# Later stores, other scratch rows and moved normalisations in a fused linear-attention and SwiGLU gradient kernel

## The chip, the cores and the metric

The kernel runs on one core of one Trainium2 chip, as one program with one launch. The metric is the device time of that program in microseconds, as the median of several runs. One further execution was taken by the hardware profiler; all views of the profile come from it.

## What is computed

The reference is one transformer block with all of its gradients. With S = 2048 tokens of width D = 640, 32 heads of 20, and a feed-forward width F = 1728, in bf16:

```python
phi = lambda t: where(t > 0, t + 1, exp(t)) + 1e-6
q, k, v = split_heads(LN(x) @ wqkv)            # LN has no weights
kv, z   = sum_s phi(k)[s] v[s]^T, sum_s phi(k)[s]
h       = x + ((phi(q) @ kv) / (phi(q) . z + 1e-6)) @ wo
y       = LN(h)
h2      = h + ((silu(y @ w_gate) * (y @ w_up)) @ w_down)
```

out_0 is h2. For a given grad_out, the outputs out_1 to out_6 are the gradients of x, wqkv (640x1920), wo, w_gate, w_up (640x1728 each) and w_down (1728x640). In what follows a name that begins with d is the gradient of the thing behind the d.

## The kernel before

**Tiles and stages.** Tokens are cut into 16 tiles of 128 rows; "tile t" means one of these, and a pair is two of them. The program has these stages, at about these times of the profiled execution:

- 0 to 141 us: the first layer norm, q and k with phi, the products that stand for kv and wo (Yt, KVT, W2), then h and the second layer norm. phi(q) is kept in DRAM as scr_pq, and the reciprocal of the denominator per token and head stays in SBUF as rall.
- 141 to 440 us: four feed-forward groups g of 448, 448, 448 and 384 columns, at 141, 214, 288 and 377 us. A group first makes gate and up (pg L792, pu L797) and their gradients pair by pair. Its gradients go transposed to scr_dT through the three "stg" buffers of the pool `small`. Then `dw_group` (L668) makes the weight gradients of those columns. The one of w_down is made transposed and stored to scr_dwdT.
- 440 to 558 us: the pair loop (L1032 to L1109), eight pairs from the last of the tokens' gradients to the attention's input, some 15.6 us each.
- 558 to 600 us: the tail behind that loop (L1110 to L1163), with the first products of G (`gt_part`).
- 600 to 627 us: the last products of G, the q part of the gradient of wqkv, and wk2 (L1227). 627 to 735 us: dk and dxn (L1280 to L1327), which end in out_1.
- 735 to 815 us: the output stage (L1453 to L1543), h2 by pairs of tiles, with the small gradients of wo and of the v part of wqkv (`dwo`, `dwv`, queue `small_q`) put between.

**Who sets the order.** Inside a `tc.manual_schedule(...)` block, the engines that it names run in the order in which the code is written; elsewhere a tile scheduler picks the order by priority and by which buffers are free. Each engine works off its own list in order, and a DMA is issued from the list of the engine that starts it, so an engine that waits for one DMA's input holds all its later DMAs. `tc.issue_after(x)` holds an instruction back in its list until behind x. Buffers come from pools: the four large strips (tag "S"), five of tag "B", three small "stg" ones, `work` (6) and `workC` (7) of one row of 640, and four PSUM tiles.

**phi(q)/den.** For G the kernel needs phi(q) times rall for all 16 tiles, as scr_pqs. `pq_load` (L635) loads tiles of scr_pq, `pq_norm` (L640) multiplies and stores. The table PQ (L646) says in which group's dw_group this is done (L729 to L750): from group g, n tiles from t0. The first five go through buffers of the feed-forward pool, further ones through stg. Before, groups 0, 1 and 2 do five, five and six tiles.

**The pair loop.** Pair p works on tiles 2p and 2p+1. The products p1, p3, p5, p6 and their relatives give the gradient of the layer norm's output (seven products where eight would do the plain way, with sums of blocks made by DVE). `ln_sum`, `ln_dot`, `ln_b` and `ln_c` (L941 to L960) do the layer norm's gradient one pair later, on tiles q2 = 2p-2 and q1 = 2p-1. `ln_c` ends with a POOL DMA that adds its result into dh1 (L957) and an SP DMA that reads that tile back transposed (dh1T, L960). `dp_mm` (L967) multiplies dh1T by W2T; `dp_a` (L975) and `dp_b` (L987) turn the result dp into dq, on tiles h-2 and f, three pairs behind. They need phi(q) again, which `load_q` (L962) loads into a stg buffer from POOL. Two tiles of scr_dwdT per pair are read back transposed on SP (dwd, L1080, buffers of workC) and stored to out_6 from POOL at the end of the same pair (L1105). Spare rows of the two tiles of transposed w_gate and w_up (`wgT`) serve as scratch: dy1 and rows pr, rx and junk.

**The tail.** Five tiles of dp work are left. They use two sets of scratch rows (L1129), so that one tile's first half runs beside the other's second half:

```python
prs, rxs = [dy1[0], pr], [junk, rx]     # dy1 and pr, rx are rows of wgT
```

`gt_part` (L907) gives the first column tiles of G = (dh1)^T pqs, over tiles t0 to t1, for one half of the columns and then for the other. `xn_act` (L999) scales rows of x, reloaded into hn (L1109, L1128), to the normalised x, on ACT, 12 tiles all told, all of them in the tail. Behind the tail wqkvT, which takes the place of one of the two wgT tiles (xnT_r takes the other), is loaded by 16 SP transposes (L1182 to L1188), held behind the last dh1T, and xnT_r by four POOL loads (L1189).

**The output stage.** Pass p of its loop (L1475) does the products of pair p and finishes pair p-1, and ends with one item of small_q except in pass 2; the rest of small_q is done behind the loop (L1522). The first item is a dwo, the other five are dwv, which need the transposes of scr_Yt into Y (L1483).

## Time and profile before

| | |
|---|---|
| time, median of 3 runs | 810.02 us (806.59 to 817.07) |
| the profiled execution: time, span | 816.33 us, 814.6 us |
| TensorE matmuls (PE) busy | 783.7 us, 96% |
| TensorE weight loads (PEld) busy | 498.8 us, 61% |
| VectorE (DVE) busy | 576.5 us, 71% |
| ScalarE (ACT) busy | 331.9 us, 41% |
| GpSimd (POOL) busy | 212.2 us, 26% |
| DMA, mean over the span | 209 GB/s |
| TensorE clock granted, mean | 0.987 |

The span is what the profiler saw of the core, from the first to the last instruction; the time has a little more around it. Weight loads run beside the matmuls. SyncE (SP) only issues DMAs here and is not counted as busy. In a timeline a row has its start in us, the busy time, the engine, the line and operation with output and input, how many instructions were merged, and in square brackets the idle time before it and what ended that. In the list of waits the numbers are the total in us, how often, and the longest one; "SPq" and "POOLq" are the DMA issues of those engines.

### The profile page before, as it was taken

To read this page: it belongs to the slowest core of one execution; us is meant where nothing else is said; L and a number is where in the kernel's file an instruction comes from. 1 tells how busy PE (TensorE), PEld (TensorE's weight loads), DVE (VectorE), ACT (ScalarE), POOL (GpSimd) and SP (SyncE) were. 2 spreads that over 40 slices of the span, in tenths; PEclk is the share of its full clock that TensorE was granted. 3 is DMA by queue.
4 is the path that set the end of the run, shared out by engine and by line. 5 is a ranking of instruction groups with operands and counts; after the bars stand their busy time and mean duration, and the time that the engine had idled before them with its cause. 6 is when DMAs were issued, how large, how long until landed. Compare 5 with 4: busy or idle time off the path is not lost.

```text
span 814.6 us, 13702 instructions
## 1 busy us (share of the span) xinstructions
PE 783.7 (96%) x5243; PEld 498.8 (61%) x5243; DVE 576.5 (71%) x1005; ACT 331.9 (41%) x490; POOL 212.2 (26%) x362
## 2 busy tenths in 40 slices
PE   9999999999999989999999999995895999999888
PEld 7776566555555545555666777773674777776555
DVE  7989988985696758757977679987561366626663
ACT  7962532840481145305701446645542133333010
POOL 4600057312311410123142133224521111123220
PEclk9999999999999999999999999998998999999989
DMA  9899999999799988995998799988669989999992
GB/s 256 173 231 317 181 260 245 262 260 229 180 225 225 182 239 215 255 184 137 215 235 240 218 204 199 249 188 232 138 115 240 164 170 170 171 248 221 203 219 82
DMA packets 291123, 170.62 MB, mean 209 GB/s; under 512 B 242396, under 2 KB 278365, under 8 KB 291056
## 3 DMA queue, kind: packets, MB, share of 16 engines
q1 hardware_dynamic: 268912, 99.56, 61.9%
q0 software_dynamic: 19248, 64.85, 28.1%
q10 hardware_dynamic: 2896, 5.33, 1.9%
q8 instruction: 41, 0.67, 0.4%
q14 instruction: 26, 0.21, 0.1%
HBM read 52.92 MB, written 56.28 MB: 134 GB/s over the span
## 4 chain that ended last, share of the span: by engine, by line
PE 84%; DMA 8%; SPq 3%; DVE 2%; ACT 2%; issue 1%; POOL 0%; POOLq 0%; ACTq 0%; DVEq 0%
PE ps_dw L871 10%; PE ps_dxn L1319 8%; PE pu L797 7%; PE ps_wa L687 7%; PE pg L792 7%; PE ps_dhn L935 6%; PE ps_dm L420 5%; PE ps_dwqk L1238 4%; PE ps_dhc L935 4%; PE ps_kq L308 4%; PE ps_oa L1389 3%; PE ps_dk L110 3%; PE ps_y L511 3%; PE ps_a L574 3%; PE ps_wc L687 2%; DMA dwd<-scr_dwdT 2%
## 5 line engine op out<-in xcount | busy, mean ns | idle before, releaser
L935 PEld LDWEIGHTS <-cols 128*128 128x128 bf16 x624 | 61.0, 98 | 24.2 <-issue 0.5
L792 PE MATMUL pg<-wgu,hnT 128*128 128x448 bf16 (+1 forms) x320 | 63.6, 346 | 1.2 <-DMA wgu<-in_B_w_gate_dram 1.2
L797 PE MATMUL pu<-wgu,hnT 128*128 128x448 bf16 (+1 forms) x320 | 63.6, 346 | 1.2 <-DMA wgu<-in_B_w_up_dram 1.2
L871 PE MATMUL ps_dw<-m_s,dh 128*128 128x448 bf16 (+1 forms) x320 | 60.4, 346 | 0.0
L1319 PEld LDWEIGHTS <-ring 128*128 128x128 bf16 x480 | 47.0, 98 | 18.2
L1319 PE MATMUL ps_dxn<-wqkvT,ring 128*128 128x320 bf16 x320 | 51.3, 299 | 0.0
L792 PEld LDWEIGHTS <-hnT 128*128 128x128 bf16 x320 | 31.2, 98 | 28.5 <-DMA wgu<-in_B_w_gate_dram 1.7
L797 PEld LDWEIGHTS <-hnT 128*128 128x128 bf16 x320 | 31.2, 98 | 28.5 <-DMA wgu<-in_B_w_up_dram 1.6
L871 PEld LDWEIGHTS <-dh 128*128 128x128 bf16 x320 | 31.3, 98 | 27.1
L420 PE MATMUL ps_dm<-wdT,dh2T 128*128 128x448 bf16 (+1 forms) x240 | 46.5, 344 | 0.0
L420 PEld LDWEIGHTS <-dh2T 128*128 128x128 bf16 x320 | 31.0, 98 | 25.1
L813 ACT ACTIVATE dd<-pg 128x896 bf16<-128x896 f32 (+1 forms) x32 | 28.5, 891 | 42.4 <-PE pg L792 42.4
L308 PE MATMUL ps_kq<-wqk,xnT 128*128 128x320 bf16 x320 | 44.8, 299 | 0.4 <-DMA xnT<-xn 0.3
L833 POOL DMA_DIRECT2D scr_m<-m_s x16 | 12.1, 756 | 125.4 <-DVE m_s L825 125.4
L1238 PEld LDWEIGHTS <-hn 128*128 128x128 bf16 x320 | 31.4, 99 | 12.8 <-issue 0.3
L308 PEld LDWEIGHTS <-xnT 128*128 128x128 bf16 x320 | 31.0, 98 | 12.8 <-DMA xnT<-xn 0.6
L687 PEld LDWEIGHTS <-S 128*128 128x128 bf16 x256 | 25.0, 98 | 21.7
L683 DVE TENSOR_TENSOR dd<-dd 128x3584 bf16<-128x3584 bf16 (+1 forms) x12 | 23.1, 1954 | 18.9 <-PE ps_wa L687 18.9
L110 PE MATMUL ps_dp<-mats,dh1T 128*128 128x320 bf16 x160 | 25.7, 310 | 10.0 <-DMA dh1T<-dh 8.0
L140 POOL TENSOR_SCALAR lnv<-mv 128x1 f32<-128x1 f32 x32 | 11.9, 373 | 89.4 <-DVE mv L136 73.5
L148 DVE CUSTOM_DVE_ANT_0 lb_a<-lb_dy,hn 128x640 bf16<-128x640 bf16 x16 | 13.2, 825 | 30.4 <-ACT lb_dy L146 30.4
L825 DVE TENSOR_TENSOR m_s<-m_s,dd 128x896 bf16<-128x896 bf16 (+1 forms) x32 | 19.4, 605 | 17.0 <-ACT m_s L818 17.0
(245 smaller groups left out, 1768.7 us busy)
## 6 DMA issues: line engine op xcount, KB each, us to landing
scr_dT<-stg SPq DMA_DIRECT2D x48, 224.0 KB, 2.9
cols<-scr_dT POOLq DMA_DIRECT2D x6, 1728.0 KB, 10.5
scr_m<-m_s POOLq DMA_DIRECT2D x12, 448.0 KB, 4.5
pq<-scr_pq POOLq DMA_DIRECT2D x32, 160.0 KB, 5.5
cols<-scr_dT ACTq DMA_DIRECT2D x2, 1728.0 KB, 10.9
scr_dT<-stg SPq DMA_DIRECT2D x16, 192.0 KB, 2.4
scr_pq<-pqa SPq DMA_DIRECT2D x4, 640.0 KB, 4.4
scr_xnT<-xnT SPq DMA_DIRECT2D x4, 640.0 KB, 5.1
```

Source lines behind the costliest of these rows:

```text
L110: nc.tensor.matmul(ps[:, ci, :320], lhsT=lhs(k), rhs=rhs(k, *NCH[ci]), start=(start and k == 0), stop=(stop and k == n - 1))
L308: nc.tensor.matmul(ps[:, ci, :320], lhsT=xnT[:, t, k, :], rhs=wqk[:, k, w0 + n0:w0 + n1], start=(k == 0), stop=(k == DT - 1))
L420: nc.tensor.matmul(ps[:, c, :w], lhsT=dh2T[:, kt, (t + c) * P:(t + c + 1) * P], rhs=wdT[:, kt, o:o + w], start=(kt == 0), stop=(kt == DT - 1))
L511: nc.tensor.matmul(ps[:, ci, :320], lhsT=xn[:, t, i * P:(i + 1) * P], rhs=pk[:, t, n0:n1], start=(t == 0), stop=(t == ST - 1))
L687: nc.tensor.matmul(out, lhsT=lhs[:, t, :], rhs=rhs[:, t, :], start=(first and t == 0), stop=(t == 7), skip_group_check=not first)
L792: nc.tensor.matmul(pg[:, c, :w], lhsT=hnT[:, kt, (t + c) * P:(t + c + 1) * P], rhs=wg[:, kt, 0:w], start=(kt == 0), stop=(kt == DT - 1))
L797: nc.tensor.matmul(pu[:, c, :w], lhsT=hnT[:, kt, (t + c) * P:(t + c + 1) * P], rhs=wg[:, kt, w:2 * w], start=(kt == 0), stop=(kt == DT - 1))
L813: sig = nc.scalar.activation(out=dg, in_=pg[:, :, :w], func=ACT.Sigmoid)
L871: nc.tensor.matmul(ps[:, c, :w], lhsT=lhs(t), rhs=rhs(t), start=(t == 0), stop=(t == ST - 1))
L935: nc.tensor.matmul(out, lhsT=lhs[:, k, :], rhs=rhs[:, k, :], start=(first and k == 0), stop=(k == HKG - 1), skip_group_check=not first)
L1238: nc.tensor.matmul(ps[:, ci, :320], lhsT=xn_r[:, t, i * P:(i + 1) * P], rhs=dq[t // 8][:, t % 8, n0:n1] if which == 0 else dk[:, t, n0:n1] ...
L1319: nc.tensor.matmul(ps[:, ci, :320], lhsT=lhs[:, i, :], rhs=rhs[:, i, n0:n1], start=(k == 0 and i == 0), stop=(k == 2 and i == DT - 1))
```

## The change

Five edits, in the order of the program:

1. phi(q)/den: group 1 does no tiles any more, group 2 does eight (5 to 12). Tiles 13 to 15 are loaded in pair 0 of the pair loop and multiplied and stored in pair 1, through stg buffers and with plain POOL DMAs.
2. The two dW_down stores of a pair move into the next pair, behind the first `ln_c` there (`store_dwd`); the last pair's go behind the first `ln_c` of the tail.
3. `xn_act` for tiles 0 to 5 moves into the last three pairs, two tiles each; 6 to 11 stay in the tail.
4. The tail's scratch rows prs and rxs are now three rows of the strip that dq's first half lies in (where the pair loop keeps s1, u2 and u3) and junk. For the first column tile of G, `gt_part` goes four token tiles at a time, alternating between the two halves of the columns.
5. In the output stage pass 3 does no item of small_q either, so that each dwv from there comes one pass later, and one more is left for behind the loop.

```diff
--- before.py
+++ after.py
@@ -632,18 +632,18 @@
 
         pq_in = {}
 
-        def pq_load(ts, own=True):
+        def pq_load(ts, own=True, dma=pool_store):
             for t in ts:
                 pq_in[t] = flat("pq") if own else small.tile([P, D], BF16, name="pq", tag="stg", bufs=3, padded_shape=[P, 7 * P])[:]
-                pool_store(pq_in[t], scr_pq_v[:, t, :])
-
-        def pq_norm(ts):
+                dma(pq_in[t], scr_pq_v[:, t, :])
+
+        def pq_norm(ts, dma=pool_store):
             for t in ts:
                 pq = pq_in.pop(t)
                 nc.vector.tensor_tensor(out=hb(pq), in0=hb(pq), in1=bc(rall[:, t, :]), op=ALU.mult)
-                pool_store(scr_pqs_v[:, t, :], pq)
-
-        PQ = {0: (0, 5), 1: (5, 5), 2: (10, 6)}
+                dma(scr_pqs_v[:, t, :], pq)
+
+        PQ = {0: (0, 5), 2: (5, 8)}
 
         wg_t = {}
 
@@ -904,9 +904,9 @@
     dh1 = dh2
     gts = {}
 
-    def gt_part(ps, i, t0, t1):
-        for ci, (n0, n1) in enumerate(NCH):
-            for t in range(t0, t1):
+    def gt_part(ps, i, t0, t1, by=ST):
+        for ci, (n0, n1), t in [(ci, n, t) for a in range(t0, t1, by) for ci, n in enumerate(NCH)
+                                for t in range(a, min(a + by, t1))]:
                 nc.tensor.matmul(ps[:, ci, :320], lhsT=dh1[:, t, i * P:(i + 1) * P], rhs=pqs_tm[:, t, n0:n1],
                                  start=(t == 0), stop=(t == ST - 1))
 
@@ -1001,6 +1001,12 @@
                 nc.scalar.activation(out=hn[:, t, :], in_=hn[:, t, :], func=ACT.Identity, scale=rstd1[:, t:t + 1],
                                      bias=nmr1[:, t:t + 1])
 
+        def store_dwd(p):
+            for i in (2 * p - 2, 2 * p - 1):
+                if i >= 0:
+                    r0 = i * P
+                    nc.gpsimd.dma_start(out=out_6[r0:min(r0 + P, F), :], in_=dwds.pop(i)[:min(P, F - r0), :])
+
         def rs(p, r):
             t = 2 * p + 1 - r
             return rstd2[:, t:t + 1]
@@ -1037,6 +1043,8 @@
             if p > 0:
                 ln_sum(q2, dy2)
                 ln_dot(q2, dy2)
+            if p == 0:
+                pq_load(range(13, ST), False, nc.gpsimd.dma_start)
             load_q(h)
             if p not in (1, 2):
                 p1(p)
@@ -1049,13 +1057,18 @@
             if p > 0:
                 ln_b(q2)
             widen(pr, nS1, h - 2)
+            if p >= NPR - 3:
+                xn_act(range(2 * (p - NPR + 3), 2 * (p - NPR + 3) + 2))
             if p > 0:
                 p3(p - 1)
                 ln_c(q2, dy2)
+                store_dwd(p - 1)
             dp_b(h - 2)
             load_q(2 * p - 3)
             if p > 0:
                 c12(p - 1)
+                if p == 1:
+                    pq_norm(range(13, ST), nc.gpsimd.dma_start)
             else:
                 nc.vector.tensor_tensor(out=T5, in0=BL[:, 0:320], in1=BL[:, 320:D], **sub)
                 nc.vector.tensor_tensor(out=T4, in0=B21, in1=T2, **sub)
@@ -1099,10 +1112,6 @@
                 p1(p + 1)
             prod(A, p, col_blk(p, 1, 1), T4, left=(1, T5))
             scaled(dy2[:, 0:320], A, p, 1)
-            if p > 0:
-                for i in (2 * p - 2, 2 * p - 1):
-                    r0 = i * P
-                    nc.gpsimd.dma_start(out=out_6[r0:min(r0 + P, F), :], in_=dwds.pop(i)[:min(P, F - r0), :])
             if p < DT:
                 tr_piece(woT, A_wo, p)
             if p in (3, 5, 7):
@@ -1118,6 +1127,7 @@
         widen(pr, nS1, ST - 6)
         c12(p)
         ln_c(ST - 2, dy2)
+        store_dwd(p)
         ln_sum(ST - 1, dy1[p % 2])
         ln_dot(ST - 1, dy1[p % 2])
         dp_b(ST - 6)
@@ -1126,7 +1136,8 @@
         load_q(ST - 3)
         last_dh1T = ln_c(ST - 1, dy1[p % 2])
         nc.gpsimd.dma_start(out=hn[:, ST - 4:ST, :], in_=x_v[:, ST - 4:ST, :])
-        prs, rxs = [dy1[0], pr], [junk, rx]
+        kb = [dqs[:, i * D:(i + 1) * D] for i in (8, 9, 10)]
+        prs, rxs = [kb[0], junk], kb[1:]
 
         def dp_1(t):
             dp_a(t, prs[t % 2])
@@ -1143,14 +1154,14 @@
         dp_1(ST - 4)
         dp_2(ST - 5)
         dp_2(ST - 4)
-        xn_act(range(0, 5))
+        xn_act(range(6, 8))
         for i, t in ((0, None), (1, ST - 3), (2, ST - 2)):
             gts[i] = mm("ps_gt")
-            gt_part(gts[i], i, 0, ST - 4)
+            gt_part(gts[i], i, 0, ST - 4, ST if i else 4)
             if t:
                 dp_mm(t)
                 dp_1(t)
-                xn_act(range(5, 7) if t == ST - 3 else range(7, 9))
+                xn_act(range(t - 5, t - 3) if t == ST - 3 else range(t - 4, t - 3))
         GT = mat(2 * DT * D, DT, D)
         ps = gts.pop(0)
         gt_part(ps, 0, ST - 4, ST)
@@ -1159,7 +1170,7 @@
         dp_mm(ST - 1)
         dp_1(ST - 1)
         dp_2(ST - 2)
-        xn_act(range(9, ST - 4))
+        xn_act(range(11, ST - 4))
         last_dq = dp_2(ST - 1)
 
     with tc.manual_schedule(engines={EngineType.SP, EngineType.DVE}):
@@ -1505,7 +1516,7 @@
                 step_f(v)
                 osum(p + 1, 1)
                 osum(p + 1, 3)
-                if p != 2:
+                if p not in (2, 3):
                     f, i = small_q.pop(0)
                     f(i)
 
```

## Prediction before the run

> **What bounds the kernel now.** First the busy table and TensorE's own waits over the whole span, then the chain of waits, then the timelines of POOL and PE around the gaps that these name.
>
> ```profile
> PE 783.7 (96%) x5243; PEld 498.8 (61%) x5243; DVE 576.5 (71%) x1005; ACT 331.9 (41%) x490; POOL 212.2 (26%) x362
> ...
> PE ps_wk L129 <- DMA wqkvT<-in_A_wqkv_dram: 8.2, 2, 7.8
> PE ps_dp L110 <- DMA dh1T<-dh: 8.0, 1, 8.0
> PE ps_dwv L129 <- DMA mats<-scr_Yt: 5.2, 2, 4.5
> PE ps_dp L110 <- ACT dp L973: 2.1, 2, 1.7
> PE pg L792 <- DMA wgu<-in_B_w_gate_dram: 1.2, 1, 1.2
> PE pu L797 <- DMA wgu<-in_B_w_up_dram: 1.2, 1, 1.2
> ```
>
> TensorE is the bound: 96% busy, 30.9 us idle in 814.6. So a change that takes no matmul away can only win those gaps, and four places hold 26 us of them: (A) 2.4 at the start of feed-forward group 2, (B) 8.0 + 2.1 behind the pair loop, (C) 8.2 at wk2, (D) 5.2 at the first dW_v. The chain of waits says what stands before B and C:
>
> ```profile
> 529.59 8.04 DMA dwd<-scr_dwdT
> 540.20 4.88 DMA pq<-scr_pq
> 558.66 9.76 DMA dwd<-scr_dwdT
> 571.02 4.69 DMA pq<-scr_pq
> 603.90 15.45 DMA wqkvT<-in_A_wqkv_dram
> ```
>
> The two dwd pieces are POOL waiting, as its timeline shows; the next two lines are SP's waits:
>
> ```profile
> 538.21 1.24 POOL L1105 DMA_DIRECT2D out_dram<-dwd  x2 [11.71 <-DMA dwd<-scr_dwdT]
> 540.73 0.92 POOL L957 DMA_DIRECT2D dh<-lb_a  x1
> 569.01 1.22 POOL L1105 DMA_DIRECT2D out_dram<-dwd  x2 [9.70 <-DMA dwd<-scr_dwdT]
> 571.55 0.93 POOL L957 DMA_DIRECT2D dh<-lb_a  x1
> ...
> SPq L960 <- DMA dh<-lb_a: 77.4, 14, 15.8
> SPq L1180 <- DVE dp L992: 18.4, 1, 18.4
> ```
>
> POOL stands 11.7 and 9.7 us in front of the dW_down stores (L1105), with pq loads and the accumulations into dh1 (L957) behind them. DVE had lb_a ready at 530.9 and 560.8; it left at 540.73 and 571.55, some 10 us late each time, so SP's dh1T transposes (L960) came late too. L1180 is SP holding the wqkvT transposes until the last dp work lets go of wgT. TensorE shows the result:
>
> ```profile
> 567.91 2.85 PE L110 MATMUL ps_dp<-mats,dh1T 128*128 128x320 bf16 x10 [7.96 <-DMA dh1T<-dh]
> 583.98 1.52 PE L110 MATMUL ps_dp<-mats,dh1T 128*128 128x320 bf16 x10 [1.68 <-ACT dp L973]
> 619.40 1.28 PE L129 MATMUL ps_wk<-mats,wqkvT 128*128 128x40 bf16 x15 [7.75 <-DMA wqkvT<-in_A_wqkv_dram]
> 775.51 0.28 PE L129 MATMUL ps_dwv<-stg,mats 128*128 128x120 bf16 x1 [4.54 <-DMA mats<-scr_Yt]
> ```
>
> The same ten matmuls take 2.85 us after the long gap and 1.52 us otherwise, so a gap costs more than its length.
>
> **What the Trainium skill says.** "TensorE: Matmul & The Clock Gate", section "What's actually happening", has the array fall to half its clock after an idle window of about 3.4 us; the trace agrees (2.85 against 1.52 us; 12 matmuls of L1389 take 3.33 us after D and 1.79 otherwise). The specification table of the same page calls the queues of ScalarE, VectorE and GpSimd strictly first in, first out; the trace agrees, L957 leaves only after L1105. "DMA: Bandwidth & Descriptors", section "Issuing engines are not separate DMA queues", says that transfers of SP, ACT and POOL interleave on the same 16 engines; the trace agrees: dh1T(12), issued at 557.31 between the pqs_tm loads, took 10.6 us to land, where the median of dh1T is 4.4. That is why traffic moved to another place is priced below.
>
> **The change part by part.**
>
> *Stores of dW_down a pair later (B).* They now stand in the next pair, behind its first accumulation. Their transposes leave about 7 us into a pair of 15.6 us and land in 3.2 us (median, 9.8 at most), so they are there when POOL comes. dh(12) should leave at about 547 instead of 553.9, dh(14) at 561 instead of 571.6, pq(12) at about 557 instead of 571.0. Won at most: 7.96 (wait) + 1.33 (2.85 against 1.52) + 0.43 (48 matmuls of L910 in 7.12 us, against 6.69 at the 0.136 us each of the later 68) + 2.08 (waits on ACT's dp) + 0.30 at 551.07: 12.1 us. Not all of it comes back. dh1T(12) now leaves near 552, while the four pqs_tm loads (640 KB each), which wait for PE at 549.5, are in flight: with the 10.6 us seen it lands at 562.6, with 4.4 at 556.4, and PE wants it at 559.95. Bounds 0 to 2.7; I take 2, short of the worst because fewer stores lie in the way. dh1T(15) comes behind the last dW_down stores, whose transposes cross the same traffic: 0 to 5, I take 2. B gives 8.1. The DVE tail stays covered: five tiles of 3.8 us (1.5 for L977 to L980, 2.3 for L991 to L997) from 564 end near 586, and PE needs 27.2 us (160 matmuls of L910 and 40 of L110 at 0.136) plus the 4 from 560, to 591.
>
> *dp work in dq's strip (C).* Both wgT tiles are free after the accumulation input of tile 15 (564), not after the last dp at 600. The 16 wqkvT transposes can follow the last dh1T, at about 574 instead of 597.4, and the xnT_r loads move up likewise. wk2 wants the first six at about 602; six issues of 1.3 us and 15.5 us of landing as seen give 597. Won: 8.16 + 1.03 (16 matmuls in 3.36 against 2.33 us) = 9.2. In the built order two xnT_r loads stand before pq(14) and one between pq(14) and pq(15); with hn's 640 KB ahead, pq(14) may land near 580 and pq(15) near 583, which the DVE tail takes within its 5 us of slack. Cost 0, up to 7 without that slack.
>
> *Normalised x in the loop.* Six ACT instructions of 0.84 us move into the last three pairs, two each, ahead of an eviction before which ACT idles 3.77 us (L1009 at 534.12): 1.7 us, covered; 0 to 0.5 a pair otherwise. In the tail it takes 5 us off ACT, which is how the waits on ACT's dp go.
>
> *phi(q)/den elsewhere (A).* Group 1 loses five loads, five stores and five DVE instructions of 0.82 us. Its wgT transposes share 266 to 284 with those loads, and the wgu loads leave only after them, at 283.6 and 284.04. 0.8 MB of loads at the 185 GB/s seen there is over 4 us of traffic: A should go, 0 to 2.4, I take 2. Group 2 gets two more instructions (1.6 us), into the 2.19 us that DVE idles before 377.59. Tiles 13 to 15: the built order puts their loads early in group 3, where they wait for stg buffers until scr_dT's last store (434.36, and 2.3 to land), and POOL's dW stores queue behind, from 415 to about 444. Nothing in that group's DVE or ACT order needs those stores; ln_dot(0) at 453.32 does, and they have landed by about 450. But over 1 MB now lies beside cols(1), issued at 437.55, landing 8.9 us later and needed at 448.89: 0 to 3 us, I take 0.5. Their three norms in pair 1 (2.4 us) fall into DVE's 2.11 us of idle before 460.09: 0 to 0.3.
>
> *dW_v a pair later (D).* The first one waits for Y's last transposes, landed at 776.4. Pair 4 first takes 6.9 us from 770.6, to 777.5, so the wait goes: 5.21 + 1.54 of clock = 6.75. What is late next is mT: DVE already waited until 772.39 for mT(9), with PSUM operands of pair 3 behind that wait (0.5 to 1), and mT(11), issued at 773.6 and landing in a median of 8.2, comes at about 782 where PE would want its sum at 781.4 (0 to 3, I take 1.5). Two dW_v now meet at the end, the second waiting for ACT's 0.69 us eviction: 0.5. D gives 4.0.
>
> Sum: A 2 + B 8.1 + C 9.2 + D 4.0 - 0.5 = 22.8. On the profiled execution: span 814.6 to 791.8, time 816.33 to 793.5. The median of the runs is 6.3 below that execution. I take it that half of the difference lies in waits that go anyhow, so that only half comes off: 793.5 - 3.2, say 790 us.
>
> **The rivals.** A measurement of this kernel can tell about 2% from no change, which puts "faster" below 793.8.
> 1. *The tail fills again.* hn, xnT_r and the wqkvT transposes are bunched into 567 to 585, pq(14), pq(15) or dh1T(15) land over 5 us later still, and dp, not PE, ends that stage: 7 us back, and 3 more at mT: 800. For it: xnT_r took 9.7 us to land. Against: DMA was 0.02 to 0.29 busy from 588 to 600, so there is room.
> 2. *wqkvT doesn't move*, because SP still waits for something near the end of the dp work: C is lost, 799. Against: the built order has no wgT in that work.
> 3. *All of it goes*: no residual of B and D: 6 to 7 us more, 784.
> 4. *Slower.* The stores now stand before a pair's second pq load, its cols load and its second accumulation. If the dwd transposes take over 12 us from issue to landing, POOL blocks in the middle of each pair, and cols comes late. At 5 us in each of six pairs this is 30 lost against 22.8: 817. The trace's 9.8 at most speaks against it.
>
> **How the numbers follow.** Forecast 0.66 (786 to 796), rival 3 0.10, rival 1 0.13, rival 2 0.05, rival 4 0.06. Under 793.8 lie five sixths of the forecast, rival 3 and a trace of rival 1: faster 0.67. The slower rival is half beyond 826: slower 0.04 with a little of wider trouble, the same 0.29. 783 to 802 leaves out rival 4, a part of rival 1 and a little at the bottom.
>
> **What would show it.** PE's waits on dh1T under 4 us, on wqkvT and scr_Yt none; POOL's waits at the dW_down stores from 65 us to under 15; wqkvT's first transpose within 5 us of the last dh1T; PE clock 1.0 from 612 to 620 of before's places; a new PE or DVE wait on mT of 1 to 3. Wrong: PE waiting for pq, dp or dh1T over 8 us in the tail, or PE idle within the pair loop.

## The result: 0.6% faster, a fifth of what was forecast

The changed kernel takes 806.18 us (median of 20 runs, 800.49 to 817.18) against 810.07 us (20 runs, 805.85 to 817.57): ratio 0.9939, 95% interval 0.9911 to 0.9968. The forecast was 790. The profiled execution took 804.86 us with a span of 803.1, against 816.33 and 814.6 before, so the two traces differ by 11.5 us and the medians by 3.9. Medians are of all runs of a kernel; ratios leave out runs over 1.5% above its fastest one, among them the profiled executions of e7_hold, g1_phi_in and g4_dwv_back, so no argument here rests on those three traces.

The busy table of the changed kernel and TensorE's waits over its whole span (total in us, times, longest):

```profile
PE 782.3 (97%) x5243; PEld 498.6 (62%) x5243; DVE 575.2 (72%) x1005; ACT 331.7 (41%) x490; POOL 211.5 (26%) x362
...
PE ps_dp L110 <- DMA dh1T<-dh: 10.1, 2, 8.9
PE ps_gt L910 <- DMA pqs_tm<-scr_pqs: 4.1, 1, 4.1
PE ps_warm L344 <- DVE ones L246: 1.1, 1, 1.1
PE ps_oa L1400 <- DVE h1r L1384: 1.0, 1, 1.0
PE ps_dwv L129 <- ACT dwv L1353: 0.8, 1, 0.8
```

Gaps A (wgu), C (wqkvT) and D (scr_Yt) are gone, and D leaves 1.8 us behind, as the last two lines say. Gap B is not gone: there were 8.0 us on dh1T and 2.1 on ACT's dp, there are now 10.1 on dh1T and 4.1 on pqs_tm. The timeline of PE behind the pair loop shows which tiles these are:

```profile
564.80 6.18 PE L910 MATMUL ps_gt<-pqs_tm,dh 128*128 128x320 bf16 x32 [4.11 <-DMA pqs_tm<-scr_pqs]
572.18 1.53 PE L110 MATMUL ps_dp<-mats,dh1T 128*128 128x320 bf16 x10 [1.20 <-DMA dh1T<-dh]
588.76 2.85 PE L110 MATMUL ps_dp<-mats,dh1T 128*128 128x320 bf16 x10 [8.94 <-DMA dh1T<-dh]
```

Before, the long wait was for tile 12; here tile 12 comes in time, 1.20 us go to tile 13, and the long wait is for tile 15, the last. The prediction had named a wait of over 8 us for dh1T in the tail as a sign of being wrong. The chain of waits (start, length in us) tells why it is late:

```profile
550.12 20.98 DMA dwd<-scr_dwdT
...
572.76 3.23 DMA dh<-lb_a
...
576.05 12.66 DMA dh1T<-dh
```

POOL's timeline has the same from the issuing side:

```profile
558.39 0.87 POOL L957 DMA_DIRECT2D dh<-lb_a  x1 [3.07 <-DVE lb_a L956]
568.73 0.56 POOL L1008 DMA_DIRECT2D out_dram<-dwd  x1 [9.48 <-DMA dwd<-scr_dwdT]
571.66 0.55 POOL L1008 DMA_DIRECT2D out_dram<-dwd  x1 [2.36 <-DMA dwd<-scr_dwdT]
572.20 0.57 POOL L965 DMA_DIRECT2D pq<-scr_pq  x1
572.76 0.92 POOL L957 DMA_DIRECT2D dh<-lb_a  x1
```

The last pair's dwd pieces took 21 us to land, with the four pqs_tm loads and a reload of x in flight. POOL stood in front of their stores until 571.7, with the accumulation into dh1(15) behind it; DVE had the input of that one at 561.4. Then the transposed read took 12.7 us, among the xnT_r loads that edit 4 pulled up. The landings of dwd's 14 transposes over the whole span (SP's DMAs alone), before and then in the changed kernel, say the same:

```profile
DMA to landing us min/median/max: 3.1/6.8/9.8
DMA to landing us min/median/max: 4.8/11.3/21.0
```

The prediction's 3.2 us for these transposes was misread: that is the median of 28 DMAs, the transposes and the 14 stores that read the same buffers. And the rise is not the last pair's alone: in pairs 1 to 5 a transpose took 4.6 to 9.1 us before and 9.2 to 13.7 in the changed kernel.

"DMA: Bandwidth & Descriptors", section "Issuing engines are not separate DMA queues", has the transfers of all issuing engines share 16 engines; this trace agrees, with SP's pieces of 160 KB at 21.0 us among POOL's loads.

### The profile page after: what moved, and what is told of

Its sections match the earlier page's. It is cut to its first block, busy times and chain, and to the rows that moved or that the text cites. A ratio compares the mean times of both kernels' runs of the same rounds, so it can differ in the third digit from the quotient of the medians.

```text
span 803.1 us, 13709 instructions
## 1 busy us (share of the span) xinstructions
PE 782.3 (97%) x5243; PEld 498.6 (62%) x5243; DVE 575.2 (72%) x1005; ACT 331.7 (41%) x490; POOL 211.5 (26%) x362
## 4 chain that ended last, share of the span: by engine, by line
PE 90%; DMA 6%; SPq 2%; DVE 1%; POOL 0%; issue 0%; ACT 0%; POOLq 0%; ACTq 0%; DVEq 0%
PE ps_dw L871 10%; PE ps_dxn L1330 8%; PE pu L797 7%; PE pg L792 7%; PE ps_wa L687 7%; PE ps_dhn L935 7%; PE ps_dwqk L1249 5%; PE ps_dm L420 5%; PE ps_dhc L935 5%; PE ps_kq L308 4%; PE ps_wc L687 3%; PE ps_dk L110 3%; PE ps_y L511 3%; PE ps_a L574 3%; DMA dwd<-scr_dwdT 3%; PE ps_oa L1400 2%
## 5 line engine op out<-in xcount | busy, mean ns | idle before, releaser
L308 PEld LDWEIGHTS <-xnT 128*128 128x128 bf16 x320 | 31.0, 98 | 12.7 <-DMA xnT<-xn 0.7
L1249 PEld LDWEIGHTS <-hn 128*128 128x128 bf16 x320 | 30.9, 98 | 12.2 <-issue 0.3
L110 PE MATMUL ps_dp<-mats,dh1T 128*128 128x320 bf16 x160 | 25.5, 310 | 10.1 <-DMA dh1T<-dh 10.1
L148 DVE CUSTOM_DVE_ANT_0 lb_a<-lb_dy,hn 128x640 bf16<-128x640 bf16 x16 | 13.2, 826 | 30.4 <-ACT lb_dy L146 30.4
L146 ACT ACTIVATE lb_dy<-ps_dxn,rstd 128x640 bf16<-128x640 f32 x16 | 12.7, 793 | 45.0 <-PE ps_dxn L1330 45.0
```

The costliest lines, as they stand in the source:

```text
L110: nc.tensor.matmul(ps[:, ci, :320], lhsT=lhs(k), rhs=rhs(k, *NCH[ci]), start=(start and k == 0), stop=(stop and k == n - 1))
L308: nc.tensor.matmul(ps[:, ci, :320], lhsT=xnT[:, t, k, :], rhs=wqk[:, k, w0 + n0:w0 + n1], start=(k == 0), stop=(k == DT - 1))
L1249: nc.tensor.matmul(ps[:, ci, :320], lhsT=xn_r[:, t, i * P:(i + 1) * P], rhs=dq[t // 8][:, t % 8, n0:n1] if which == 0 else dk[:, t, n0:n1] ...
```

## The experiments

Ratios are to the kernel before, from runs on the same chip, with 95% intervals. The stages are of one execution each. For many kernels the span is split in three, from the starts of TensorE's tiles: to the first matmul of the pair loop; from there to the first of dk, which holds gaps B and C; from there to the start of the last matmul, which holds D.

| kernel | ratio | to the loop | loop to dk | dk to the end |
|---|---|---|---|---|
| before | 1 | 439.8 | 187.2 | 184.2 |
| changed | 0.9939 (0.9911 to 0.9968) | 437.5 | 183.1 | 179.1 |
| e1_stores | 0.9985 (0.995 to 1.002) | 437.2 | 182.8 | 187.2 |
| e2_strip | 0.9973 (0.9939 to 1.0006) | 437.7 | 185.5 | 182.1 |
| e3_phi | 1.0055 (1.0018 to 1.0093) | 437.4 | 193.9 | 178.2 |
| e4_dwv | 1.0027 (1.0005 to 1.005) | 439.2 | 188.7 | 178.0 |
| e5_last_stores | 0.9928 (0.9899 to 0.9958) | 437.8 | 186.3 | 177.9 |
| e6_no_phi | 0.995 (0.9923 to 0.9977) | 438.7 | 179.0 | 178.0 |
| e7_hold | 0.9887 (0.9834 to 0.994) | | | |
| e8_three | 0.9876 (0.9835 to 0.9917) | 437.7 | 180.5 | 180.8 |
| f1_late | 0.9859 (0.9816 to 0.9902) | 437.6 | 174.4 | 179.7 |
| f2_pair_end | 0.9941 (0.9905 to 0.9977) | 443.3 | 180.7 | 177.9 |
| f3_dwv_back | 0.9874 (0.983 to 0.9919) | 436.8 | 177.2 | 177.0 |
| f4_both | 0.975 (0.9712 to 0.9787) | 437.5 | 168.3 | 177.9 |
| g2_x_early | 0.9769 (0.9714 to 0.9824) | 437.2 | 172.0 | 182.2 |
| g3_no_hold | 0.972 (0.9669 to 0.9771) | 438.1 | 166.6 | 178.0 |
| g5_dwd_early | 0.9796 (0.9755 to 0.9837) | 437.5 | 174.5 | 178.0 |
| g6_own_pair | 0.9786 (0.9728 to 0.9843) | 438.6 | 174.0 | 185.7 |

### Each large edit alone

**e1_stores**: before, with edit 2 alone.

```diff
                 ln_c(q2, dy2)
+                store_dwd(p - 1)
...
-            if p > 0:
-                for i in (2 * p - 2, 2 * p - 1):
-                    r0 = i * P
-                    nc.gpsimd.dma_start(out=out_6[r0:min(r0 + P, F), :], in_=dwds.pop(i)[:min(P, F - r0), :])
...
         ln_c(ST - 2, dy2)
+        store_dwd(p)
```

> The kernel before with edit 2 alone: dW_down stored a pair later. Theory (the last pair's pieces are the fault): the two dwd transposes of pair 7 leave at about 549 among the four pqs_tm loads and the hn load and take 15 to 21 us to land, as in the changed kernel; the last two stores hold the accumulation into dh1(15) until about 570, TensorE waits 5 to 9 us for dh1T(15) in place of the 8.0 for dh1T(12), and the time stays within 3 us of before. Rival (the tail is choked only by what edit 4 pulls forward): without xnT_r and wqkvT nearby these two land in under 10 us, waits on dh1T come to under 3 us, and the time falls by 7 to 10 us.

Measured 808.93 us, no change that can be told. The last pair's dwd pieces took 16.2 and 15.8 us to land among the pqs_tm loads and a reload of x, so the loads that edit 4 pulls up are not needed for that. (The longest landing, 17.3 us, was in the middle of the loop, of a piece that left at 520.50.) POOL's timeline:

```profile
565.92 0.56 POOL L1008 DMA_DIRECT2D out_dram<-dwd  x1 [6.87 <-DMA dwd<-scr_dwdT]
567.48 0.55 POOL L1008 DMA_DIRECT2D out_dram<-dwd  x1 [0.99 <-DMA dwd<-scr_dwdT]
568.02 0.57 POOL L965 DMA_DIRECT2D pq<-scr_pq  x1
568.60 0.92 POOL L957 DMA_DIRECT2D dh<-lb_a  x1
```

The accumulation into dh1(15) was held to 568.6. But TensorE waited only 2.7 us for dh1T: with xnT_r far off, that tile landed in time.

**e2_strip**: before, with edit 4 alone.

```diff
-        prs, rxs = [dy1[0], pr], [junk, rx]
+        kb = [dqs[:, i * D:(i + 1) * D] for i in (8, 9, 10)]
+        prs, rxs = [kb[0], junk], kb[1:]
...
-            gt_part(gts[i], i, 0, ST - 4)
+            gt_part(gts[i], i, 0, ST - 4, ST if i else 4)
```

> The kernel before with edit 4 alone: the tail's scratch in dq's strip, and gt_part four tiles at a time for its first column tile. Theory: the wait on wqkvT (8.2 us, and 1.0 of half clock) goes and nothing takes its place, since the stores are out of POOL before; 6 to 9 us faster than before. Rival (edit 4 chokes the tail): xnT_r and wqkvT push dh1T(15) or the last two phi(q) loads over 5 us later, TensorE waits for dp work, and the gain is under 3 us.

Measured 807.34 us, within the error of no change. Here the rival is right. TensorE's waits:

```profile
PE ps_dp L110 <- DMA dh1T<-dh: 13.1, 3, 6.8
PE ps_dwv L129 <- DMA mats<-scr_Yt: 3.2, 2, 2.9
PE ps_dwqk L1239 <- DVE hn L1256: 1.6, 1, 1.6
```

No wait on wqkvT is left, and two on dh1T stand in its place: 5.8 us for tile 12, as before, and 6.8 us for tile 14, which was in time before. The xnT_r loads left from 570.41 on, right behind the accumulations, and the phi(q) load of tile 15 took 21.3 us by the chain of waits (3.4 at the median in before's tail).

**e3_phi**: before, with edit 1 alone.

```diff
-        PQ = {0: (0, 5), 1: (5, 5), 2: (10, 6)}
+        PQ = {0: (0, 5), 2: (5, 8)}
...
+            if p == 0:
+                pq_load(range(13, ST), False, nc.gpsimd.dma_start)
...
+                if p == 1:
+                    pq_norm(range(13, ST), nc.gpsimd.dma_start)
```

> The kernel before with edit 1 alone: phi(q)/den of group 1 moved to group 2 and into the pair loop. Theory: the two waits on wgu at the start of group 2 (2.4 us) go and nothing else moves, 2 to 3 us faster. Rival: the loads of tiles 13 to 15 in group 3, waiting for stg buffers, hold POOL and cost it back: no gain.

Measured 815.01 us, slower, and more than the rival had. POOL's timeline in group 3:

```profile
436.36 0.54 POOL L638 DMA_DIRECT2D pq<-scr_pq  x1 [24.52 <-DMA scr_dT<-stg]
444.93 0.54 POOL L638 DMA_DIRECT2D pq<-scr_pq  x1 [8.03 <-issue]
445.71 0.54 POOL L638 DMA_DIRECT2D pq<-scr_pq  x1 [0.24 <-issue]
446.24 1.08 POOL L875 DMA_DIRECT2D out_dram<-dwev  x2
```

POOL stands over 30 us before the loads of tiles 13 to 15, 24.5 of them for a stg buffer, and the weight gradients' stores leave 13 to 31 us later than before. The next cols load stands behind them in POOL's list: it left at 455.70 where before it left at 448.55, and TensorE waited 3.8 us for it in the loop.

**e4_dwv**: before, with edit 5 alone.

```diff
-                if p != 2:
+                if p not in (2, 3):
```

> The kernel before with edit 5 alone: dwv one pass later from pass 3. Theory: the wait on scr_Yt (5.2 us and 1.5 of half clock) goes, 1 to 2 us come back at h1r and at the last dwv: 4 to 6 us faster on the profiled execution. Rival: the wait that goes is one that most executions don't have (the profiled one is 6 us above its median), and the medians differ by under 2 us.

Measured 809.6 us: nothing won, and with an interval of 1.0005 to 1.005 the 4 us of the prediction are excluded. Its profile has no wait on scr_Yt, but it need not have had one: with the output stage unchanged, that wait is 5.2 us in before, 6.9 in e1_stores, 3.2 in e2_strip, 0.8 in e3_phi. The wait on wgu is the same sort of thing: e1_stores, e2_strip, e4_dwv and ten of the kernels further down (those without edit 1) have the code of before up to there, and none of their traces shows it.

### Taking the tail apart

**e5_last_stores**: the changed kernel, with the last two stores moved.

```diff
         ln_c(ST - 2, dy2)
-        store_dwd(p)
...
         nc.gpsimd.dma_start(out=hn[:, ST - 4:ST, :], in_=x_v[:, ST - 4:ST, :])
+        store_dwd(p)
```

> The changed kernel, with the last two dW_down stores and nothing else moved: behind the accumulation into dh1(15) and the last reload of x. Theory (the blocked store is what makes dh1T(15) late): the accumulation leaves at about 562 instead of 572.8, dh1T(15) lands before TensorE wants it near 580, the wait of 8.9 us and its 1.3 us of half clock go, and the time falls 7 to 10 us against the changed kernel, to 797 to 799. Rival (the loads pulled forward fill the DMA engines and make it late wherever it starts): dh1T(15) still lands at 584 or later, and under 4 us are won.

Measured 805.54 us, 0.9928, as the changed kernel: the rival. The accumulation into dh1(15) left at 562.07, but TensorE still waited 5.5 us for dh1T(15), 5.0 for another dh1T and 5.1 for pqs_tm. So the blocked store is not needed for dh1T(15) to be late: its transposed read left at 573.87, among the xnT_r and wqkvT loads, and took 17.9 us.

**e6_no_phi**: the changed kernel without edit 1.

```diff
-        PQ = {0: (0, 5), 2: (5, 8)}
+        PQ = {0: (0, 5), 1: (5, 5), 2: (10, 6)}
...
```

> The changed kernel with edit 1 taken back: phi(q)/den in groups 0, 1 and 2 again. Edit 1 alone had measured 1.0055 of before. Theory (the three loads that wait for stg buffers in group 3 hold POOL for 17 to 25 us and push DMA traffic into the pair loop, and the wgu wait that edit 1 was to remove is absent in most executions): 3 to 5 us faster than the changed kernel, 801 to 803. Rival (with the other edits in, edit 1's late traffic is harmless, as the one profile without a wait on cols suggests): within 2 us of the changed kernel or slower.

Measured 806.42 us, 0.995: the rival. What edit 1 costs alone it doesn't cost here. Why is open; POOL's longest stand at L638 was 16.7 us in the changed kernel and 24.5 in e3_phi.

**e7_hold**: the changed kernel, xnT_r held.

```diff
-        dp_mm(ST - 1)
+        last_dp = dp_mm(ST - 1)
...
-            pool_load(xnT_r[:, 4 * c:4 * c + 4], scr_xnT[4 * c:4 * c + 4].rearrange("t p k c -> p t k c"))
+            wait_for(last_dp, [nc.gpsimd.dma_start(out=xnT_r[:, 4 * c:4 * c + 4],
+                                                   in_=scr_xnT[4 * c:4 * c + 4].rearrange("t p k c -> p t k c"))])
```

> The changed kernel with the four xnT_r loads held until dp of tile 15 has left TensorE, so that they don't stand beside dh1T(15). Theory that the traffic of these loads is what slows dh1T(15) (12.7 us to land in the changed kernel): it lands in about 5 us, at 581 instead of 588.8, TensorE's wait shrinks from 8.9 to under 2 us, and 6 to 9 us are won. Rival, that the late start behind the blocked stores alone counts: it lands in over 9 us also without them, since the wqkvT transposes and the reload of x remain, and under 3 us are won.

Measured 801.05 us, 0.9887; its interval touches that of the changed kernel, so it hints at 4 us and shows none.

**e8_three**: the edits of e5_last_stores, e6_no_phi and e7_hold together.

> All three together: the changed kernel without edit 1, with the last stores behind the accumulation into dh1(15), and with the xnT_r loads held until dp of tile 15. If edit 1 costs 4 us and the tail's wait of 10 us goes: 791 to 795, and TensorE's waits in the tail are the one on pqs_tm (4 us) and little else. If TensorE's idle time only moves (xnT_r or wqkvT late for dk or wk2): 798 to 804.

Measured 802.31 us, 0.9876: better than the changed kernel by less than hoped. In its trace dh1T(15) took 6.1 us to land and is in time, but TensorE stood 8.3 us for dh1T(13), whose accumulation and transposed read took 9.8 and 10.9 us among pqs_tm, x and dwd. And now there is a stall within the loop. POOL's timeline of e8_three near 510 us:

```profile
507.62 0.56 POOL L1008 DMA_DIRECT2D out_dram<-dwd  x1 [8.75 <-DMA dwd<-scr_dwdT]
510.75 0.55 POOL L1008 DMA_DIRECT2D out_dram<-dwd  x1 [2.58 <-DMA dwd<-scr_dwdT]
511.29 0.54 POOL L965 DMA_DIRECT2D pq<-scr_pq  x1
511.83 0.71 POOL L162 DMA_DIRECT2D cols<-scr_dT  x1
512.53 0.93 POOL L957 DMA_DIRECT2D dh<-lb_a  x1
```

The stores stand 11 us in front of pq, cols and the pair's second accumulation; TensorE stood 3.2 us a little later (523.39, for DVE's dp work). That is the place where edit 2 put them. The two transposes that they wait for took 21.2 and 22.1 us to land, and the cols load that left beside them 17.5, where in f4_both further down it took 8.1 and the transposes under 7.

### Two moves that only work together

**f1_late**: e8_three, with both reloads of x and the last dwd pieces started only behind the accumulation into dh1(15), the stores at the very end of the tail, and `xn_act` of tiles 8 to 11 behind the dp work. `load_dwd` holds the two dwd transposes.

```diff
-            if p > 0:
+            if 0 < p < NPR - 1:
+                load_dwd(p)
...
-            if p in (3, 5, 7):
+            if p in (3, 5):
...
-        nc.gpsimd.dma_start(out=hn[:, ST - 4:ST, :], in_=x_v[:, ST - 4:ST, :])
-        store_dwd(p)
+        nc.gpsimd.dma_start(out=hn[:, ST - 8:ST - 4, :], in_=x_v[:, ST - 8:ST - 4, :])
+        load_dwd(p)
...
-                xn_act(range(t - 5, t - 3) if t == ST - 3 else range(t - 4, t - 3))
...
-        xn_act(range(11, ST - 4))
+        xn_act(range(8, ST - 4))
         last_dq = dp_2(ST - 1)
+        nc.gpsimd.dma_start(out=hn[:, ST - 4:ST, :], in_=x_v[:, ST - 4:ST, :])
+        store_dwd(p)
```

> e8_three with more traffic taken out of the 20 us behind the pair loop: both reloads of x and the last two dwd pieces start only behind the accumulation into dh1(15), and xn_act for tiles 8 to 11 goes to the end of the tail. Theory (the stretch is limited by what the DMA engines have to move, so each accumulation and dh1T lands late in it): the waits of TensorE on dh1T and pqs_tm fall from the 8 to 14 us of the earlier kernels to under 5, and the median from 802.3 to 796 to 799. Rival (what is left there, pqs_tm with 2.6 MB, is enough by itself): waits of 7 us or more stay, and the median is within 2 us of 802.

Measured 798.81 us, 0.9859. TensorE's waits on dh1T and pqs_tm came down to 5.5 us, near the 5 of the theory. By the ratios, 0.9859 against 0.9876, no gain over e8_three can be told: the two ran on different chips, so their medians don't compare.

**f2_pair_end**: e8_three, with the loop's stores behind the second accumulation of the next pair.

```diff
                 ln_c(q2, dy2)
-                store_dwd(p - 1)
...
                 ln_c(q1, dy1[(p - 1) % 2])
+                store_dwd(p - 1)
```

> e8_three with the dW_down stores of a pair behind the second accumulation of the next pair instead of the first. In the profiled execution of e7_hold POOL stood 15.9 us before a store in the middle of a pair and TensorE then 8.7 us for dh1T. If that happens in many executions: POOL's waits before stores no longer hold an accumulation, the loop has no wait on dh1T, the slow end of the runs (over 805) thins out and the median falls 2 to 4 us. If it is rare, or the transposes themselves are slow because the engines are full: within 2 us of e8_three.

Measured 805.84 us, 0.9941: no gain. POOL's waits in front of stores fell to 2.2 us in all, but TensorE still waited 8.2 us for dh1T and 3.5 for pqs_tm behind the loop. (This execution was also 5.6 us longer than e8_three's ahead of the loop, where the code is the same.)

**f3_dwv_back**: e8_three without edit 5.

```diff
-                if p not in (2, 3):
+                if p != 2:
```

> e8_three without edit 5 (the first dwv in pass 3 again). If the wait on scr_Yt that the first profile showed is a matter of that execution, as the 0.8 to 6.9 us in kernels with the same output stage and the unchanged median of e4_dwv suggest: within 2 us of e8_three, either way. If the wait is typical: 4 to 6 us slower than e8_three.

Measured 799.75 us, 0.9874 against 0.9876. No gain from edit 5 can be told, though with intervals of this width one of 4 us could hide, and no wait on scr_Yt is in this profile.

**f4_both**: f1_late and f2_pair_end together.

> f1_late and f2_pair_end together, as the candidate for the fastest. If both reasons hold: 793 to 797. If neither: 801 to 803.

Measured 790.33 us, 0.975: the fastest so far, below what either expectation had, and its six runs lie between 788.96 and 792.04. Its busy table and waits:

```profile
PE 777.9 (99%) x5243; PEld 496.7 (63%) x5243; DVE 577.0 (73%) x1005; ACT 331.7 (42%) x490; POOL 211.6 (27%) x362
...
PE ps_dp L110 <- ACT dp L973: 3.4, 2, 3.0
PE ps_warm L344 <- DVE ones L246: 1.1, 1, 1.1
PE ps_dwv L129 <- ACT dwv L1353: 0.8, 1, 0.8
PE ps_wc L687 <- DVE dd L683: 0.6, 1, 0.6
```

No DMA is left in that list. POOL's timeline has the cols load that left at 511.83 in e8_three 12 us earlier, and the stores don't wait:

```profile
499.97 0.72 POOL L162 DMA_DIRECT2D cols<-scr_dT  x1
505.69 0.89 POOL L957 DMA_DIRECT2D dh<-lb_a  x1 [5.00 <-DVE lb_a L956]
506.28 1.40 POOL L1013 DMA_DIRECT2D out_dram<-dwd  x2
```

The intervals of f1_late and f2_pair_end are apart from that of f4_both. So with the tail's traffic moved, the place of the stores in the loop is worth 1.1%, and with the stores at the pair's end, the tail's traffic is worth 1.9%.

### Undoing one part of f4_both

The kernel before ran at 814.39 us beside the first four and at 816.07 beside the last two, so only the ratios compare with 0.975. f4_both itself was not run on that chip.

**g1_phi_in**, with edit 1:

```diff
-        PQ = {0: (0, 5), 1: (5, 5), 2: (10, 6)}
+        PQ = {0: (0, 5), 2: (5, 8)}
...
```

> f4_both with edit 1 put back in. Theory (POOL held 17 to 25 us in group 3 by three loads that wait for stg buffers, and what it queues there reaches the pair loop, as e3_phi measured with +0.55%): 3 to 6 us slower than f4_both, 793 to 796. Rival (harmless where the rest has slack, as e6_no_phi against the changed kernel showed): within 1 us, 789 to 791.

797.34 us, 0.976 (0.9708 to 0.9813): no cost that can be told.

**g3_no_hold**, without the wait on xnT_r:

```diff
-            wait_for(last_dp, [nc.gpsimd.dma_start(out=xnT_r[:, 4 * c:4 * c + 4],
-                                                   in_=scr_xnT[4 * c:4 * c + 4].rearrange("t p k c -> p t k c"))])
+            pool_load(xnT_r[:, 4 * c:4 * c + 4], scr_xnT[4 * c:4 * c + 4].rearrange("t p k c -> p t k c"))
```

> f4_both without the wait on the xnT_r loads. Theory (2.6 MB that start beside dh1T(15) and the wqkvT transposes fill the DMA engines): TensorE waits 4 us or more for dh1T(15) or wqkvT, 794 to 800, and the runs spread wider. Rival (with x and dwd out of the way there is room for them): within 1.5 us of f4_both.

794.13 us, 0.972 (0.9669 to 0.9771): no cost either. In its trace the first xnT_r load leaves at 564.11, between the last transposed reads of dh1, and TensorE waits 1.4 us for dh1T in all: with x and dwd out of the way there was room. The runs spread over 787 to 808.

**g4_dwv_back**, without edit 5:

```diff
-                if p not in (2, 3):
+                if p != 2:
```

> f4_both without edit 5. If the wait on scr_Yt is a matter of single executions: 788 to 791, and the two dwv that meet at the end cost edit 5 about 1 us, so this is 0 to 1 us faster. If it is typical once the kernel ahead of it is steady: 3 to 6 us slower, 793 to 796.

796.03 us, 0.9752 (0.9701 to 0.9804): no gain from edit 5 can be told here either.

**g5_dwd_early**, the last dwd pieces in their pair:

```diff
-            if 0 < p < NPR - 1:
+            if p > 0:
                 load_dwd(p)
```

> f4_both with the last pair's two dwd transposes back in that pair, so among the pqs_tm loads. They landed after 15 to 23 us there. Theory (they and pqs_tm slow each other and the dh1T transposes behind them on SP): TensorE waits 3 us or more on pqs_tm or dh1T, 793 to 797. Rival (only a store that waits for them hurt, and it is behind everything now): within 1.5 us of f4_both.

797.52 us, 0.9796 (0.9755 to 0.9837). The trace follows the theory, dwd at 19.7 us and TensorE waiting 3.4 us on pqs_tm and 4.8 on dh1T, though no store stands in the way; the ratio hints at 0.5%, and the intervals overlap.

**g2_x_early**, the reloads of x where the changed kernel has them:

```diff
-            if p in (3, 5):
+            if p in (3, 5, 7):
...
-        nc.gpsimd.dma_start(out=hn[:, ST - 8:ST - 4, :], in_=x_v[:, ST - 8:ST - 4, :])
+        nc.gpsimd.dma_start(out=hn[:, ST - 4:ST, :], in_=x_v[:, ST - 4:ST, :])
...
```

> f4_both with the two reloads of x (1.3 MB) and xn_act of tiles 8 to 11 back where the changed kernel has them. Theory (they stand beside pqs_tm and the last accumulations and slow both): TensorE waits 3 to 8 us on dh1T or pqs_tm, 794 to 799. Rival (they have room): within 1.5 us of f4_both.

794.17 us, 0.9769 (0.9714 to 0.9824): not told apart. Its trace speaks for the rival, with 0.4 us of waits on dh1T and none on pqs_tm.

**g6_own_pair**, stores at the end of their own pair, as before:

```diff
                 ln_c(q1, dy1[(p - 1) % 2])
-                store_dwd(p - 1)
...
+            if p < NPR - 1:
+                store_dwd(p)
```

> f4_both with the dW_down stores of each pair at the end of that pair again, as in the kernel before, so edit 2 undone but for the last pair. Theory (before, POOL stood 65 us in front of these stores, and each accumulation and dh1T was up to 10 us late): dh1T waits come back within the loop or at its end, 793 to 798. Rival (the lateness before hurt only through pqs_tm and the last pair's pieces, which stay moved): within 1.5 us of f4_both.

796.19 us, 0.9786 (0.9728 to 0.9843): not told apart by time. In its profile POOL stands 52.6 us in front of the stores, and TensorE waits 8.0 us for dh1T behind the loop, which f4_both has not.

## Why the prediction was wrong, step by step

Of the 16.2 us between 790 and 806.18, 11.4 are missing in the profiled execution (793.5 forecast, 804.86 measured), and 4.8 between that execution and the median (3.5 below it forecast, 1.3 above it measured). The first part is B's: too little was kept for what lands late behind the loop. The second goes with A and D.

**The busy table, and that only gaps can be won: right.** PE's busy time hardly moved, and f4_both, with its gaps closed, is at 99%.

**A (2 us) and D (4 us): the step that failed is to price a wait that one execution shows as if each had it.** In the two traces both went: the start of the loop came 2.3 us earlier and the part from dk on is 5.1 us shorter. In the medians no gain is left of D: e4_dwv has 1.0027, and e8_three and f3_dwv_back, f4_both and g4_dwv_back are equal within 0.1%, with intervals of 0.4 to 0.5% to each side. A's wait stands in the trace of before alone, and no kernel with edit 1 gained measurably on the same one without it. The profiled execution of before stood 6.3 us above its median. Only half of that was taken off on the way to the median; A and D in that execution, 7.6 us of waits and 1.5 of half clock, are more than all of it. That fits: e1_stores, e2_strip and e3_phi, with 6.9, 3.2 and 0.8 us of waits on scr_Yt, were profiled 3.4 and 3.1 us above and 0.3 below their medians. How often an execution has these waits is not on record.

**B (8.1 us): the step that failed in the trace; two terms were mis-sized, and one is missing.** "Their transposes leave about 7 us into a pair of 15.6 us and land in 3.2 us (median, 9.8 at most), so they are there when POOL comes": the 3.2 us are misread (6.8 for the transposes alone), and both are of before. In the changed kernel the loop's pieces took up to 13.7 us and the last pair's 19.4 and 21.0 among pqs_tm. "dh1T(15) ... 0 to 5, I take 2": it was 8.94 us, with 1.33 of half clock. POOL's waits in front of the stores fell from 65.0 us to 30.9 and not to under 15. dh1T(12), for which 2 us were kept, is in time, and tile 13 costs 1.20; pqs_tm, for which PE waited 4.11 us and ran at half clock after it, was not in the sum at all, since its loads were counted as what slows others and not as what PE waits for next.

**C (9.2 us): the mechanism was right, the path behind it wrong.** The first wqkvT transpose left at 577.36, right behind the last dh1T, and the wait on it is gone. But e2_strip shows that the same release lets xnT_r start beside the last transposed reads of dh1, and 6.8 us come back there. It is not those loads alone: in g3_no_hold they start as early, with x and dwd moved, and the waits on dh1T are 1.4 us. "Against: DMA was 0.02 to 0.29 busy from 588 to 600, so there is room" looked at the stretch that the traffic leaves; it went into 560 to 588, where the engines were already 0.81 busy in the trace of before.

The tail accounts for the profiled execution. Behind the loop PE waited 4.11 + 1.20 + 8.94 us and lost 1.33 and 1.7 to half clock (the second is 32 matmuls in 6.18 us that take 4.5 at 0.136 each), 17.2 in all, where the sum had left 4. The stage from the loop to dk shows the same: 4.1 us won where B and C were to give 17.3, so 13.2 short. The other stages won 7.4 us where 5.5 were forecast, which leaves the 11.4.

**Normalised x and edit 1:** no wait of dp on ACT remains in the changed kernel's list, as said. Edit 1's cost had been put at 0.5 us; alone it measured 0.55%, some 4 us, in a trace in which POOL stood over 30 us at L638. In combination it cost nothing, which is not explained.

**The rivals.** Rival 1 named what happened: hn, xnT_r and wqkvT bunched up, dh1T(15) late, DMA and not PE ending the stage; it had 800 against a median of 806, as it kept the gains of A and D. Rival 4's mechanism, stores that block POOL in the middle of a pair, is in e8_three's trace, and the place of the stores is worth the 1.1% between f1_late and f4_both (POOL stands 41.9 us in front of them in f1_late's trace and not at all in f4_both's): under 9 us of the 30 that rival 4 gave it, and outweighed by the gains elsewhere. Its condition, over 12 us from issue to landing, came true: the changed kernel's loop had 13.7, against the 9.8 that had spoken against it.

What stays open: which of f4_both's parts carries it. Each single one of six, taken back, costs 0.5% at most, within the errors. In single traces the stage from the loop to dk is 6 us longer with the dwd pieces early or the stores in their own pair, and no longer without the hold on xnT_r (168.3 against 174.5, 174.0 and 166.6). And the pieces do not add up: on top of e8_three, one half of the moves gives 0.2%, the other none, and both give 1.3%.

## What to carry to other kernels

A wait in one profile is a sample: before it is priced, set the profiled execution against the median of the runs, and look whether another kernel with the same code there has the wait. When an edit lets transfers start earlier, add up what is in flight in the stretch that they move into, on all queues, and ask for the tile that lands last there. A store that may have to wait for its input belongs behind everything in its queue that another engine waits for, and here the free queue and the free stretch together gave what neither had given alone. With f4_both's stores back in their own pair no loss could be told, so that is not shown to be a rule.

## What was not expected of the hardware

A transposed dwd piece (160 KB) landed in 6.8 us before (median of 14, 9.8 at most). The last pair's two took 15.5 to 20.8 us (means of the two) in the eight kernels e1_stores, e5_last_stores, e6_no_phi, e8_three, f2_pair_end, f3_dwv_back, g5_dwd_early and the changed one, where they start among the pqs_tm loads. Behind the last accumulation they took 3.9 to 4.2 us in f1_late, f4_both, g2_x_early and g6_own_pair, and 8.6 in g3_no_hold, where xnT_r is not held. The bytes alone do not explain it: in the changed kernel 257 GB/s moved from 550 to 560 us and 127 to 179 from 560 to 569, with the engines' busy share at 1.0 or more throughout. What slows them is not shown.

The place of the stores in POOL's list goes with the time that the transposes ahead of them take. In pairs 1 to 6 the longest landing of a dwd piece is 13.7 to 23.4 us in the seven traces with the stores behind the first accumulation of the next pair (the changed kernel, e1_stores, e5_last_stores, e6_no_phi, e8_three, f1_late, f3_dwv_back), and 7.9 to 11.5 us in the ten with them elsewhere. So POOL waited there for transposes that had become slow, and not only for ones that it met early. Why they become slow is open, and the place is not the whole of it: g1_phi_in and g4_dwv_back, in the executions left out above, have 28.3 and 19.9 us with the stores at the pair's end.

The length of a gap does not tell whether TensorE's clock drops. "TensorE: Matmul & The Clock Gate", section "What's actually happening", has that happen after an idle window of about 3.4 us. In the traces read here every gap of 3.5 us or more was followed by matmuls at half clock, but shorter ones went both ways. In f1_late ten matmuls behind a gap of 2.79 us take 2.85 us:

```profile
573.24 2.85 PE L110 MATMUL ps_dp<-mats,dh1T 128*128 128x320 bf16 x10 [2.79 <-DMA dh1T<-dh]
```

In e8_three, behind 3.24 us, they take 1.53:

```profile
523.39 1.53 PE L110 MATMUL ps_dp<-mats,dh1T 128*128 128x320 bf16 x10 [3.24 <-DVE wgT L991]
```

After 1.96 us in e1_stores they took 2.34, and after 2.98 in f4_both 1.52. So a gap of 2 to 3.4 us cannot be priced by its length.
